# Chunked attention and a gated layer on one core: in token blocks 1 and 2, products with v and the next scores inserted as one piece

## The chip, the core and the metric

The kernel runs on one core of one Trainium2 chip. The time is that of the device, in microseconds (us); the median of three runs is given with its lowest and highest. The profile is one further execution, taken by the hardware profiler. Its span runs from the first to the last instruction that it shows. Engines are called as in the profile: PE (TensorE, matmul), PEld (its weight loads), DVE (VectorE), ACT (ScalarE), POOL (GpSimd), SP (SyncE, which issues all DMAs here).

## The reference

```python
# q, k, v: (8 batches, 8 heads, 576, 64), cut into chunks of 64 rows: plain softmax attention within each chunk
scores = scale * np.matmul(q_c, k_c.transpose(0, 1, 2, 4, 3))
scores = scores - np.max(scores, axis=-1, keepdims=True)
attn = np.exp(scores)
attn = attn / (np.sum(attn, axis=-1, keepdims=True) + 1e-09)
out = np.matmul(attn, v_c)
# x: all heads side by side, 4608 tokens x 512
gate = 1.0 / (1.0 + np.exp(-(x @ w_gate)))      # w_gate, w_val: 512 x 1536
val = x @ w_val
return (gate * val @ w_out).astype(np.float32)  # w_out: 1536 x 512
```

## The kernel before

**Work.** The 4608 tokens are nine blocks m of 512. Attention is cut into 36 units j, four to a block, and two units make a pair (j, j+1). For a pair, PE makes the scores (`products`, tile `sc`, L171), DVE takes the maximum and subtracts it (L535, L536 in `flow`), ACT takes the exponential, DVE sums and divides (L557 to L562) and transposes the 32x32 squares into `pbd` with 16 instructions (L575 in `spread`), PE multiplies by v (`values`, tile `av`, L232), and ACT copies the result out of PSUM (L243; for blocks 0 to 2 ACT and DVE split it into two parts, L250 and L251).

**Layer.** Each matmul is done in three products of high and low parts. Blocks 0, 1 and 2 go singly. For each of the 12 slices f of the hidden width, `hidden` runs 12 matmuls of the gate layer into the PSUM bank `g0` and 12 of the value layer into the bank `g1` (both are tile `g`, L262). DVE multiplies out of `g1` (L273, tile `hf`), ACT casts the product to its high part (`hh`, L275), DVE makes the low part (`hl`, L277). `down` then runs 12 matmuls of the slice before (tile `acc`, L288: four token tiles t, three matmuls each). After the last slice of a block, each token tile is copied out (`ob` or `obs`; even t on DVE, L308, odd t on ACT, L306) and stored (L309). In block 1 all four copies go through `ob`, which has two buffers: tile t=2 needs the buffer that t=0 is stored from.

Blocks 3 to 8 go in three stages n of two blocks, with seven products in place of eight for the up layers. `operands` makes the seven operands B11, B21, T1, B22, T3, T2, T4 of a stage: four differences (L401, on DVE), seven casts to the high part (L403, ACT) and seven low parts (L412, DVE; 128x1024). `first`, `middle` and `last` run the products in the PSUM tiles `cx`, `cy`, `cz` (L422); `cx` and `cy` use the banks of `acc`. A stage ends with `outward` (L503).

**Order.** On PE and DVE the code order is the order of the instructions (`manual_schedule`). ACT's and SP's is made by the framework's scheduler. The attention of pair j from 8 on is a generator, `flow`, which stops at items: a number is DVE work of that size, "S", "A" and "AS" are insertions on PE, "wait" lets at least some ticks pass. After each layer step, `rest` calls `tick` (which hands `flow` a share of DVE time, `SHARES`, and runs its DVE work up to it) and `insert` (which runs a due insertion). `step(m, f)` issues the up layers of slice f, `finish()` the down matmuls of the slice before. `due(n, k)` forces `flow` on until k operands exist.

**Insertions.** With `joined` false, the scores of pair j ("S") and the products with v of pair j-2 ("A") are two insertions at different places, all through the two PSUM banks `psa`. With `joined` true they are one ("AS"): the two `av` first, then `sc` of j into the bank `g1` (`apart`), then `sc` of j+1 into `psa`. Before the change `joined` becomes true at stage 0, which is after block 2.

Of the kernel before, what the change touches and what calls it, by code (L numbers as in the profile page):

```python
# [41 lines left out]
FIRST_PAIR = 3  # L42


SHARES = {1: 2.5, 2: 2.8, "up": 1.15, "down": 1.3}


@with_exitstack
def chunk_attn_moe(ctx: ExitStack, tc: tile.TileContext, q, k, v, w, out):
# [460 lines left out]
    def flow():  # L510


        kept = None
        for j in range(8, 4 * NB + 2, 2):
            more = j < 4 * NB
            joined = now["joined"]
            if more and joined:
                yield from spread(*kept, range(12, 16))
                yield "AS"
                values(j - 2), values(j - 1)  # L520
                scv = [products(j, True), products(j + 1)]
                load_values(j), load_values(j + 1)
            elif more:
                yield "S"
                scv = [products(j), products(j + 1)]
            if more:
                if j + 2 < 4 * NB:
                    load(j + 2), load(j + 3)
                if kept and not joined:
                    yield from spread(*kept, range(12, 16))  # L530
                pr = ap2.tile([P, 2, 8, D], F32, name="pr", bufs=1)
                for i in range(2):
                    yield 1.4
                    mx = sm.tile([P, 8], F32, name="mx")
                    nc.vector.reduce_max(out=mx, in_=scv[i], axis=AX.X)  # L535
                    nc.vector.tensor_tensor(  # L536
                        out=pr[:, i], in0=scv[i], in1=mx.unsqueeze(2).broadcast_to([P, 8, D]), op=ALU.subtract)
                pr = pr.rearrange("p u g k -> p (u g) k")
                nc.scalar.activation(pr, pr, AF.Exp, scale=0.125)
            elif kept:  # L540
                yield from spread(*kept, range(12, 16))
            if kept and not (more and joined):
                yield "A"
                values(j - 2), values(j - 1)
                if more:
                    load_values(j), load_values(j + 1)
            else:
                yield "wait"
            n, rest = divmod(j - 4 * FIRST_PAIR, 8)
            if n > 0 and rest == 0:  # L550
                yield ("open", n - 1)
                yield from operands(n - 1)
            if not more:
                return
            yield 1.5
            sums = sm.tile([P, 16], F32, name="sums2", bufs=1)
            nc.vector.reduce_sum(out=sums, in_=pr, axis=AX.X)  # L557
            nc.vector.tensor_scalar_add(out=sums, in0=sums, scalar1=1e-9)
            inv = sm.tile([P, 16], F32, name="inv2", bufs=1)
            nc.vector.reciprocal(out=inv, in_=sums)  # L560
            yield 1.2
            nc.vector.tensor_tensor(out=pr, in0=pr, in1=inv.unsqueeze(2).broadcast_to([P, 16, D]), op=ALU.mult)  # L562
            kept = pr, pbd2
            yield from spread(*kept, range(12))

    def spread(pr, pb, which):

        ps = pr.rearrange("p g (k j) -> p g k j", j=32)
        pb = pb.rearrange("p u (x c) h (i q) -> p (u x) c h i q", c=2, q=32)
        for n in which:  # L570
            c, i, h, k = n >> 3, n >> 2 & 1, n >> 1 & 1, n & 1
            src = slice((2 * c + i) * 32, (2 * c + i + 1) * 32)
            dst = slice((2 * h + k) * 32, (2 * h + k + 1) * 32)
            yield 0.44
            nc.vector.transpose(out=pb[dst, :, c, h, i, :], in_=ps[src, h::2, k, :])  # L575

    ahead = flow()
    now = dict(credit=0.0, ticks=0, since=0, unit=8, open=-1, joined=False)
    now["item"] = next(ahead)

    def advance():
        now["unit"] += 2 * (now["item"] in ("A", "AS"))
        now["item"] = next(ahead, None)
        now["since"] = now["ticks"]

    def tick(share):
        now["ticks"] += 1
        now["credit"] += share
        while now["item"] is not None:
            if isinstance(now["item"], float):  # L590
                if now["credit"] < now["item"] / 2:
                    return
                now["credit"] -= now["item"]
            elif not (now["item"] == "wait" and now["ticks"] > now["since"] + 1
                      or now["item"][0] == "open" and now["item"][1] <= now["open"]):
                break
            advance()
        now["credit"] = min(now["credit"], share)

    def insert(upto=4 * NB, pieces=0):  # L600


        if now["item"] == "S" or (
                now["item"] in ("A", "AS") and now["unit"] < upto and now["ticks"] >= now["since"] + pieces):
            advance()
# [42 lines left out]
    kept = [(p, which, c) for p in range(6) for which in range(2) for c in range(2)]  # L648
# [7 lines left out]
                keep_sums(p, which, c)  # L656

    def rest():
        for m in range(1, FIRST_PAIR):
            upto = 4 * (m + 2) if m == 1 else 4 * (m + 3)  # L660
            for f in range(2 if m == 1 else 0, NF):
                if m == 2 and f == 7:
                    now["open"] = 0
                step(m, f, "")
                tick(SHARES[m])
                insert(upto, 2)
                finish()
                tick(SHARES[m])
                insert(upto, 2)
                if m == 1:  # L670
                    keep_outer(f)
                    if f == 11:
                        keep_outer(0), keep_outer(1)

                keep(24 - len(kept), (7 * (12 * m + f - 13)) // 5)
                if m == 2:
                    if f == 8:
                        for which in range(2):
                            load_group(0, 0, which)
        for n in range(3):  # L680
            m0 = FIRST_PAIR + 2 * n
            upto = 4 * NB
            now["joined"] = True
            order = [(p, which) for p in range(6) for which in range(2)]
            due(n, 6)
            for i, (p, which) in enumerate(order):
                if i + 1 < len(order) and i > 0:
                    load_group(n, *order[i + 1])
                if pending:
                    banks[n, "z"] = sole(n, p, which)  # L690
                    while pending:
                        finish()
                first(n, p, which)
                tick(SHARES["up"] if i > 1 else 0)
                if i:
                    due(n, 7)
                    last(n, *order[i - 1])
                    tick(SHARES["up"] if i < 11 else 0)
                    insert(upto, 1)
                middle(n, p, which)  # L700
                tick(SHARES["up"] if 0 < i < 11 else 0)
                insert(upto, 1)
            load_outer(0), load_outer(1)
            parts = split(n, 0, 0)
            last(n, *order[-1])
            now["open"] = n + 1
            for b in range(2):
                for f in range(NF):
                    if f % 2 == 0:
                        later = 6 * b + f // 2 + 2  # L710
                        if later < 12:
                            load_outer(later % 6)
                        elif n + 1 < 3:
                            load_group(n + 1, 0, later - 12)
                    hh, hl = parts if f == 0 else split(n, f, b)
                    if (b, f) != (0, 0):
                        tick(SHARES["down"])
                    if (b, f) == (0, NF - 1):
                        parts = split(n, 0, 1)
                    if (n, b) == (2, 1) and f >= NF - 2:  # L720
                        pending.append((f, hh, hl))
                        continue
                    for t in range(4):
                        outward(m0 + b, f, t, hh, hl)
                    if (b, f) not in ((0, NF - 2), (0, NF - 1)):
                        insert(upto, 1)

        for i, tiles in ((0, (0, 1, 2)), (1, (0,)), (0, (3,)), (1, (1, 2, 3))):
            f, hh, hl = pending[i]
            for t in tiles:  # L730
                outward(NB - 1, f, t, hh, hl)
# [34 lines left out]
```

## Time and profile before

| | |
|---|---|
| median of 3 runs | 940.39 us (940.23 to 942.07) |
| profiled execution | 941.31 us, its span 939.5 us |
| PE busy | 924.0 us, 98% of the span, granted clock 0.993 on average |
| DVE, ACT, POOL busy | 64%, 36%, 14% |
| mean DMA traffic | 202 GB/s |

A busy PE is the sum of intervals in which a matmul is under way. They overlap, so what one more matmul costs is read from the distance of starts, not from its duration. The profile's times count from the start of the span.

### The profile page before, as it was taken

What the parts mean: (1) busy time and instruction counts of PE and PEld (TensorE: products, weight loads), DVE (VectorE), ACT (ScalarE), POOL (GpSimd) and SP (SyncE); (2) the same over time, 40 slices, a digit from 0 to 9 for tenths busy, and PEclk for the clock granted to TensorE, in tenths of its full rate; (3) what the DMA queues carried; (4) which work ended last, traced back from release to release, by engine and by line L of the source; (5) the groups of instructions that cost most, each with busy time, mean ns of one, the idle gap of its engine ahead of it and who ended that gap; (6) DMA issues with size and microseconds to landing.
All of it is one profiled execution on the core that took longest, in us unless ns stands there. A gap on an engine that the chain in (4) does not pass through costs nothing.

```text
span 939.5 us, 13059 instructions
## 1 busy us (share of the span) xinstructions
PE 924.0 (98%) x4960; PEld 762.5 (81%) x4960; DVE 602.0 (64%) x999; ACT 339.8 (36%) x554; POOL 135.1 (14%) x204
## 2 busy tenths in 40 slices
PE   6999999999999999999999999999999999999998
PEld 4788888888888888888888888888888888888886
DVE  6999973666576656866867556786866735455332
ACT  6899753233233342231323431233232421121222
POOL 1000006997069700000000000000000000000000
PEclk7999999999999999999999999999999999999999
DMA  8699885444343464576775756666656465556561
GB/s 275 219 308 293 314 297 198 135 135 129 101 153 125 139 197 157 171 227 209 232 246 201 272 201 200 199 218 223 214 202 236 165 215 185 207 176 217 211 225 45
DMA packets 81279, 189.61 MB, mean 202 GB/s; under 512 B 7488, under 2 KB 38208, under 8 KB 76608
## 3 DMA queue, kind: packets, MB, share of 16 engines
q1 hardware_dynamic: 81216, 188.77, 60.0%
q8 instruction: 39, 0.64, 0.3%
q14 instruction: 24, 0.20, 0.1%
HBM read 150.99 MB, written 37.75 MB: 201 GB/s over the span
## 4 chain that ended last, share of the span: by engine, by line
PE 87%; DVE 4%; DMA 4%; ACT 3%; issue 1%; SPq 1%; ACTq 0%; DVEq 0%
PE acc L503 21%; PE cy L422 16%; PE g L262 15%; PE cz L422 10%; PE cx L422 10%; PE acc L288 8%; PE sc L171 3%; PE av L232 3%; DMA w_raw<-w_in 3%; DMA kbd<-k_in 1%; DVE w L137 1%; DVE w_raw L132 1%; ACT w_raw L129 1%; DVE w_raw L134 1%; ACT w_raw L130 1%
## 5 line engine op out<-in xcount | busy, mean ns | idle before, releaser
L262 PE MATMUL g<-xt,w 128*128 128x512 f32 (+1 forms) x960 | 207.6, 371 | 2.3 <-ACT w L136 0.9
L262 PEld LDWEIGHTS g<-xt,w 128*128 128x128 f32 x960 | 168.5, 189 | 35.7 <-issue 1.7
L503 PE MATMUL acc<-wr,hh 128*128 128x512 f32 x576 | 178.0, 390 | 0.0
L422 PE MATMUL cy<-xc,wr 128*128 128x512 f32 x648 | 160.2, 390 | 0.0
L422 PEld LDWEIGHTS cy<-xc,wr 128*128 128x128 f32 x648 | 121.3, 188 | 25.7 <-issue 0.7
L503 PEld LDWEIGHTS acc<-wr,hh 128*128 128x128 f32 x576 | 107.7, 188 | 23.4 <-ACT hh L493 1.0
L503 PE MATMUL acc<-wr,hl 128*128 128x512 f32 x288 | 112.4, 390 | 0.0
L422 PE MATMUL cz<-xc,wr 128*128 128x512 f32 x432 | 109.7, 389 | 0.0
L422 PE MATMUL cx<-xc,wr 128*128 128x512 f32 x432 | 105.0, 389 | 0.0
L575 DVE STREAM_TRANSPOSE pbd<-pr 32x256 f32<-32x256 f32 x224 | 97.7, 436 | 4.5 <-DVE pr L562 0.5
L495 DVE TENSOR_TENSOR hl<-hid,hh 128x512 fp32r<-128x512 f32 x72 | 49.6, 690 | 72.5 <-ACT hh L493 67.5
L422 PEld LDWEIGHTS cz<-xc,wr 128*128 128x128 f32 x432 | 81.0, 188 | 17.2 <-DVE u L479 0.4
L422 PEld LDWEIGHTS cx<-xc,wr 128*128 128x128 f32 x432 | 81.0, 188 | 16.9 <-issue 0.2
L288 PE MATMUL acc<-w,hh 128*128 128x512 f32 x288 | 90.4, 395 | 0.0
L493 ACT CAST hh<-hid 128x512 fp32r<-128x512 f32 x72 | 44.6, 620 | 115.1 <-PE acc L503 84.6
L273 DVE TENSOR_TENSOR hf<-g,hf 128x512 f32<-128x512 f32 (+1 forms) x40 | 25.4, 635 | 62.8 <-PE g L262 62.7
L503 PEld LDWEIGHTS acc<-wr,hl 128*128 128x128 f32 x288 | 54.1, 188 | 12.5 <-DVE hl L495 1.3
L339 POOL TENSOR_TENSOR a_val<-w 128x256 f32<-128x256 f32 x48 | 38.4, 820 | 178.6 <-ACT hh L275 143.0
L440 DVE TENSOR_TENSOR u<-cy,s 128x512 f32<-128x512 f32 x36 | 24.9, 691 | 61.1 <-PE cy L422 61.1
L288 PEld LDWEIGHTS acc<-w,hh 128*128 128x128 f32 x288 | 52.7, 188 | 12.1 <-issue 1.7
L288 PE MATMUL acc<-w,hl 128*128 128x512 f32 x144 | 56.1, 389 | 0.0
L271 ACT ACTIVATE hf<-g 128x512 f32<-128x512 f32 (+1 forms) x40 | 22.1, 554 | 76.6 <-PE g L262 75.3
(103 smaller groups left out, 1003.5 us busy)
## 6 DMA issues: line engine op xcount, KB each, us to landing
wr<-sums SPq DMA_DIRECT2D x72, 512.0 KB, 4.5
wr<-outer SPq DMA_DIRECT2D x36, 1024.0 KB, 4.9
w_raw<-w_in SPq DMA_DIRECT2D x36, 512.0 KB, 5.8
wr<-given SPq DMA_DIRECT2D x36, 512.0 KB, 3.7
sums<-a_both SPq DMA_DIRECT2D x24, 512.0 KB, 3.5
qt<-q_in SPq DMA_DIRECT2D x36, 256.0 KB, 4.5
kbd<-k_in SPq DMA_DIRECT2D x72, 128.0 KB, 4.4
vt<-v_in SPq DMA_DIRECT2D x36, 256.0 KB, 4.3
```

The costliest lines, as they stand in the source:

```text
L171: nc.tensor.matmul(sc[c * D:(c + 1) * D, (2 * a + t) * P:(2 * a + t + 1) * P], lhsT=s["qt"][:, a, n0:n0 + D], rhs=s["kb"][:, a, :, n0:n0 + D],
L232: nc.tensor.matmul(av[a * D:(a + 1) * D, c * P:(c + 1) * P], lhsT=s["vt"][:, a, c, :], rhs=pb[:, 4 * a + c, :, :], start=True, stop=True,)
L262: nc.tensor.matmul(ps[:, tok], lhsT=wt[f, which][:, wpart, c:c + P], rhs=x[:, part, i, tok], start=n == 0, stop=n == 11)
L273: nc.vector.tensor_tensor(out=hf, in0=pv, in1=hf, op=ALU.mult)
L288: nc.tensor.matmul(acc[m, t], lhsT=hx[:, ts], rhs=wt[f, 2][:, wpart], start=f == 0 and i == 0, stop=f == NF - 1 and i == 2,)
L339: nc.gpsimd.tensor_tensor(out=val[:, 2 * n:2 * n + 2], in0=parts[:, 0], in1=parts[:, 1], op=ALU.add)
L422: nc.tensor.matmul(bank, lhsT=lhs(wpart, c), rhs=x[:, part, c], start=start and k == 0, stop=stop and k == 5, skip_group_check=True)
L440: nc.vector.tensor_tensor(out=u2, in0=y, in1=s1, op=ALU.add)
L493: nc.scalar.copy(hh, h)
L495: nc.vector.tensor_tensor(out=hl, in0=h, in1=hh.bitcast(F32), op=ALU.subtract)
L503: nc.tensor.matmul(acc[m, t], lhsT=hx[:, ts], rhs=wo[f][:, wpart], start=f == 0 and i == 0, stop=f == NF - 1 and i == 2)
L575: nc.vector.transpose(out=pb[dst, :, c, h, i, :], in_=ps[src, h::2, k, :])
```

## The change

In blocks 1 and 2, too, `flow` joins the insertions from the second pair on (the first, j = 8, has no pair ahead of it and stays an "S"). `insert` is called once per slice, between `step` and `finish`, and an insertion may follow the one before after one tick in place of two. In these blocks a "wait" is passed one tick sooner (`lag`). The share of block 1 goes from 2.5 to 2.8.

```diff
-SHARES = {1: 2.5, 2: 2.8, "up": 1.15, "down": 1.3}
+SHARES = {1: 2.8, 2: 2.8, "up": 1.15, "down": 1.3}
...
-            joined = now["joined"]
+            joined = now["joined"] and kept
...
-            elif not (now["item"] == "wait" and now["ticks"] > now["since"] + 1
+            elif not (now["item"] == "wait" and now["ticks"] > now["since"] + now["lag"]
...
     def rest():
+        now["joined"] = True
         for m in range(1, FIRST_PAIR):
...
                 step(m, f, "")
                 tick(SHARES[m])
-                insert(upto, 2)
+                insert(upto, 1)
                 finish()
                 tick(SHARES[m])
-                insert(upto, 2)
...
-            now["joined"] = True
+            now["lag"] = 1
```

On PE the six pairs j = 10 to 20 change: twelve insertions become six. The three places below are those where other engines' rows matter; numbers behind a tile's name tell instances apart.

**First place: the end of block 1.** DVE in the kernel before, from the first slice of block 2 (`g_2579`) to the second (`g_2692`); the two L308 copy out block 1's token tiles 0 and 2:

```order
L273 TENSOR_TENSOR hf<-g_2579,hf 128x512
L277 TENSOR_TENSOR hl<-hf,hh 128x512
L308 COPY ob<-acc 128x512 x2
L557 TENSOR_REDUCE sums_2647<-pr 128x16
L558 TENSOR_SCALAR sums_2647<-sums_2647 128x16
L560 RECIPROCAL inv_2650<-sums_2647 128x16
L562 TENSOR_TENSOR pr<-pr,inv_2650 128x1024
L575 STREAM_TRANSPOSE pbd<-pr 32x8x32 x7
L273 TENSOR_TENSOR hf<-g_2692,hf 128x512
```

and in the changed kernel (the same slices are `g_2545` and `g_2679`):

```order
L273 TENSOR_TENSOR hf<-g_2545,hf 128x512
L277 TENSOR_TENSOR hl<-hf,hh 128x512
L308 COPY ob<-acc 128x512 x2
L535 TENSOR_REDUCE mx<-sc 128x8
L536 TENSOR_TENSOR pr<-sc,mx 128x512
L535 TENSOR_REDUCE mx<-sc 128x8
L536 TENSOR_TENSOR pr<-sc,mx 128x512
L273 TENSOR_TENSOR hf<-g_2679,hf 128x512
```

What followed the two copies was work on `pr`; now it is the reading of the scores, the first pair of which lies in the bank `g1` that `g_2679` is to be written to. SP at this place in the changed kernel (in the kernel before, the two `vt` loads stand directly ahead of the four stores):

```order
L158 DMA vt<-v_in 128x512 x2
L149 DMA qt<-q_in 128x512
L152 DMA kbd_87<-k_in 64x2x256 x2
L149 DMA qt<-q_in 128x512
L152 DMA kbd_88<-k_in 64x2x256 x2
L309 DMA out<-ob 128x512 x4
```

Six loads of q and k for the next pair now stand ahead of the stores of block 1, too.

**Second place: the end of block 2.** DVE in the kernel before, from the low part of slice 10 to that of slice 11 and on; L412 and L401 make the operands of stage 0:

```order
L277 TENSOR_TENSOR hl<-hf,hh 128x512
L412 TENSOR_TENSOR xc<-raw,xc 128x1024
L401 TENSOR_TENSOR raw<-raw 128x2x512
L412 TENSOR_TENSOR xc<-raw,xc 128x1024
L401 TENSOR_TENSOR raw<-raw 128x2x512
L273 TENSOR_TENSOR hf<-g_3536,hf 128x512
L277 TENSOR_TENSOR hl<-hf,hh 128x512
L412 TENSOR_TENSOR xc<-raw,xc 128x1024
L308 COPY ob<-acc 128x512
L308 COPY obs<-acc 128x512
```

and in the changed kernel, from the operands behind slice 10's low part on:

```order
L412 TENSOR_TENSOR xc<-raw,xc 128x1024
L401 TENSOR_TENSOR raw<-raw 128x2x512
L412 TENSOR_TENSOR xc<-raw,xc 128x1024 x2
L401 TENSOR_TENSOR raw<-raw 128x2x512
L412 TENSOR_TENSOR xc<-raw,xc 128x1024
L401 TENSOR_TENSOR raw<-raw 128x2x512
L273 TENSOR_TENSOR hf<-g_3532,hf 128x512
L277 TENSOR_TENSOR hl<-hf,hh 128x512
L412 TENSOR_TENSOR xc<-raw,xc 128x1024
L401 TENSOR_TENSOR raw<-raw 128x2x512
L412 TENSOR_TENSOR xc<-raw,xc 128x1024
L308 COPY ob<-acc 128x512
```

Seven operand instructions, where there were four, now stand ahead of slice 11's product, and three, where there was one, between its low part and the copies. ACT there in the changed kernel, from slice 11's sigmoid to the copies of token tiles 3 and 1 (before, `obs` and `ob` stood the other way round, and the last L403 ahead of L275):

```order
L271 ACTIVATE hf<-g_3517 128x512
L403 CAST xc<-raw 128x1024 x2
L275 CAST hh<-hf 128x512
L403 CAST xc<-raw 128x1024
L306 COPY obs<-acc 128x512
L306 COPY ob<-acc 128x512
```

**Third place: the first group of stage 0.** DVE in the kernel before, from the first L440 to the second; the L412 is the low part of T4:

```order
L440 TENSOR_TENSOR u_3613<-cy,s_3605 128x512
L412 TENSOR_TENSOR xc<-raw,xc 128x1024
L557 TENSOR_REDUCE sums_3616<-pr 128x16
L558 TENSOR_SCALAR sums_3616<-sums_3616 128x16
L560 RECIPROCAL inv_3619<-sums_3616 128x16
L462 TENSOR_TENSOR u_3635<-cy,s_3605 128x512
L464 TENSOR_TENSOR hid<-cz,u_3635 128x512
L440 TENSOR_TENSOR u_3661<-cy,s_3653 128x512
```

and in the changed kernel:

```order
L440 TENSOR_TENSOR u_3613<-cy,s_3605 128x512
L462 TENSOR_TENSOR u_3629<-cy,s_3605 128x512
L464 TENSOR_TENSOR hid<-cz,u_3629 128x512
L440 TENSOR_TENSOR u_3655<-cy,s_3647 128x512
L412 TENSOR_TENSOR xc<-raw,xc 128x1024
```

The low part of T4 now stands behind the second L440. It does so at the start of stage 1 as well.

## Rows read from the trace of the kernel before

**Rows 1.** The page: PE's busy time, share of the span and instructions, and the chain that ended last, by engine.

```profile
PE 924.0 (98%) x4960; PEld 762.5 (81%) x4960; DVE 602.0 (64%) x999; ACT 339.8 (36%) x554; POOL 135.1 (14%) x204
...
PE 87%; DVE 4%; DMA 4%; ACT 3%; issue 1%; SPq 1%; ACTq 0%; DVEq 0%
```

**Rows 2.** Instructions of PE in order of time, block 1: starts of up layers (24 matmuls). Between the first two stand only the 12 down matmuls; between the second and the third two slices, with an "S" in them; between the third and the last one slice and the "A" shown. Columns: start, duration, engine, line, operation.

```profile
166.00 5.60 PE L262 MATMUL g<-xt,w 128*128 128x512 f32 x24
...
174.16 5.60 PE L262 MATMUL g<-xt,w 128*128 128x512 f32 x24
...
192.60 5.60 PE L262 MATMUL g<-xt,w 128*128 128x512 f32 x24
198.13 1.97 PE L232 MATMUL av<-pbd,vt 128*64 128x128 f32 x32
...
202.88 5.60 PE L262 MATMUL g<-xt,w 128*128 128x512 f32 x24
```

**Rows 3.** The same view in stage 0, around an "AS" (the scores are left out).

```profile
437.69 1.52 PE L422 MATMUL cy<-xc,wr 128*128 128x512 f32 x6
439.14 1.97 PE L232 MATMUL av<-pbd,vt 128*64 128x128 f32 x32
...
442.79 1.65 PE L422 MATMUL cy<-xc,wr 128*128 128x512 f32 x6
444.28 1.52 PE L422 MATMUL cz<-xc,wr 128*128 128x512 f32 x6
445.64 2.88 PE L422 MATMUL cx<-xc,wr 128*128 128x512 f32 x12
```

**Rows 4.** Instructions of DVE in order of time, block 1: the low parts of an "A" (its `av` is that of rows 2).

```profile
200.29 1.28 DVE L251 TENSOR_TENSOR xt<-av,xt 128x512 fp32r<-128x512 f32 x2
```

**Rows 5.** The end of block 1 in order of time: PE's first matmuls after the "A" and the next up layers, DVE's two copies (in brackets: idle time before, and what ended it), SP's issue of the four stores, and a maximum and subtraction of scores on DVE shortly before.

```profile
255.57 1.97 PE L232 MATMUL av<-pbd,vt 128*64 128x128 f32 x32
257.47 0.73 PE L288 MATMUL acc<-w,hh 128*128 128x512 f32 x2
...
260.32 5.60 PE L262 MATMUL g<-xt,w 128*128 128x512 f32 x24
...
258.52 0.69 DVE L308 COPY ob<-acc 128x512 f32<-128x512 f32 x1 [0.71 <-PE acc L288]
261.54 0.69 DVE L308 COPY ob<-acc 128x512 f32<-128x512 f32 x1 [2.33 <-DMA out<-ob]
262.15 1.21 DVE L557 TENSOR_REDUCE sums<-pr 128x16 f32<-128x1024 f32 x1
...
259.24 3.86 SPq L309 DMA_DIRECT2D out<-ob  x4
...
251.50 0.69 DVE L535 TENSOR_REDUCE mx<-sc 128x8 f32<-128x512 f32 x1
252.22 0.69 DVE L536 TENSOR_TENSOR pr<-sc,mx 128x512 f32<-128x512 f32 x1
```

**Rows 6.** The loads behind an "AS" of stage 0: its start on PE, SP's first and last issue; and the page's medians from issue to landing.

```profile
400.97 1.97 PE L232 MATMUL av<-pbd,vt 128*64 128x128 f32 x32
...
402.11 1.21 SPq L158 DMA_DIRECT2D vt<-v_in  x2
...
406.10 1.18 SPq L152 DMA_DIRECT2D kbd<-k_in  x2
...
kbd<-k_in SPq DMA_DIRECT2D x72, 128.0 KB, 4.4
...
out<-ob SPq DMA_DIRECT2D x22, 256.0 KB, 2.2
```

**Rows 7.** The end of block 2 in order of time: DVE from slice 10's low part on, ACT's cast and copy, and PE from the last down matmuls to the first `cx`.

```profile
353.56 0.69 DVE L277 TENSOR_TENSOR hl<-hf,hh 128x512 fp32r<-128x512 f32 x1 [0.69 <-ACT hh L275]
354.17 1.22 DVE L412 TENSOR_TENSOR xc<-raw,xc 128x1024 fp32r<-128x1024 f32 x1
...
357.70 1.22 DVE L401 TENSOR_TENSOR raw<-raw 128x1024 f32<-128x1024 f32 x1
360.35 0.69 DVE L273 TENSOR_TENSOR hf<-g,hf 128x512 f32<-128x512 f32 x1 [1.43 <-PE g L262]
...
359.00 1.05 ACT L403 CAST xc<-raw 128x1024 fp32r<-128x1024 f32 x1 [0.77 <-DVE raw L401]
361.07 0.62 ACT L275 CAST hh<-hf 128x512 fp32r<-128x512 f32 x1 [1.02 <-DVE hf L273]
365.76 0.59 ACT L306 COPY ob<-acc 128x512 f32<-128x512 f32 x1 [4.07 <-PE acc L288]
...
364.16 0.61 PE L288 MATMUL acc<-w,hh 128*128 128x512 f32 x2
...
366.88 1.52 PE L422 MATMUL cx<-xc,wr 128*128 128x512 f32 x6
```

**Rows 8.** Stage 0 in order of time: the second L440 on DVE, and on PE the product of `last` with T4 (its first six matmuls).

```profile
375.31 0.69 DVE L440 TENSOR_TENSOR u<-cy,s 128x512 f32<-128x512 f32 x1 [0.72 <-PE cy L422]
...
376.40 2.88 PE L422 MATMUL cy<-xc,wr 128*128 128x512 f32 x12
```

**Rows 9.** Block 2 on DVE in order of time, with POOL at work: from a product out of `g1` to the first transposes behind it.

```profile
284.46 0.69 DVE L273 TENSOR_TENSOR hf<-g,hf 128x512 f32<-128x512 f32 x1 [4.08 <-PE g L262]
...
291.10 3.13 DVE L575 STREAM_TRANSPOSE pbd<-pr 32x256 f32<-32x256 f32 x7 [0.46 <-DVE pr L562]
```

More of the change, by code (lines that the diff above doesn't have):

```diff
@@ L577, in chunk_attn_moe @@
     ahead = flow()
-    now = dict(credit=0.0, ticks=0, since=0, unit=8, open=-1, joined=False)
+    now = dict(credit=0.0, ticks=0, since=0, unit=8, open=-1, joined=False, lag=0)
     now["item"] = next(ahead)
```

## The prediction

> **What bounds the kernel.** First the page: PE is busy for 924.0 of 939.5 us, and the chain that ended last runs on PE for 87% of its length [rows 1]. A change gains by what it takes off PE's own line of matmuls, and loses by every wait that it puts into that line. Second, PE in order of time, for what an insertion costs now. Third, DVE, ACT and SP around the ends of blocks 1 and 2, where they have least time to spare.
>
> **Terms on PE.** One slice (24 up and 12 down matmuls) takes 174.16 - 166.00 = 8.16 us [rows 2], so 12 matmuls take 2.72. Two slices and an "S" take 192.60 - 174.16 = 18.44, so the "S" costs 18.44 - 16.32 = 2.12; a slice and an "A" take 202.88 - 192.60 = 10.28, so the "A" costs 2.12 as well. An "AS" in stage 0 stands between two groups of six matmuls, each 445.64 - 444.28 = 1.36 long: 444.28 - 437.69 - 2 x 1.36 = 3.87 [rows 3]. The joined pair saves 2 x 2.12 - 3.87 = 0.37 us, being changed into and out of once in place of twice. Six pairs: -2.2 us. The rest of PE's work stays; the "AS" that follow in stage 0 shift by some groups and cost the same there.
>
> **Copies inside the joined piece.** The scores of j+1 use the `psa` bank that the first `av` leaves. For j = 10 and 12 that `av` belongs to block 2 and is read by ACT and then by DVE (L251). Before, L251 starts 200.29 - 198.13 = 2.16 us after its `av` [rows 2, 4] and takes 1.28 for two, so the first ends about 2.8 after; the second scores would start at some three quarters of 442.79 - 439.14 = 3.65 [rows 3], 2.7 after. I take 0.2 us for each of the two, between nothing and 0.3 (DVE's low part of the slice, ahead of L251, grows when POOL is busy): +0.4.
>
> **End of block 1.** Count from the start of the first `av`, now 3.65 us ahead of the down matmuls in place of 257.47 - 255.57 = 1.90 [rows 5]. These last 260.32 - 257.47 = 2.85, the gate layer 2.72 more, so PE wants `g1` at 3.65 + 2.85 + 2.72 = 9.22. DVE has to read the first scores out of it before, and does so only behind both L308. The first L308 starts 258.52 - 257.47 = 1.05 after the down matmuls, at 4.70, and its store could go 0.72 later, at 5.42. But SP now issues the loads of q and k ahead of it; in stage 0 the same loads end 406.10 + 1.18 - 400.97 = 6.31 after the `av` [rows 6]. So the store goes at 6.35. The second L308 began 261.54 - 259.24 = 2.30 after the issue of the store whose buffer it needs [rows 5]: 8.65, if the loads ahead don't slow it. A `kbd` load lands 4.4 us after its issue, a store in 2.2 [rows 6]; the last `kbd` is issued at about 5.7 and lands between 8.0 and 10.1, and the store of 256 KB behind it a little later. I take 9.2 for the second L308 (bounds 8.65 and 10.7, the latter with a load's 4.4 us for the store), as it is nearer to the store's own row. Then 0.61 to the next instruction, 1.41 for a maximum and a subtraction (252.22 + 0.69 - 251.50): `g1` is free at 11.2, and PE stands for 2.0 us, bounds 1.5 and 3.5. Now 2.33 us of waiting for the store hold up only sums that nobody wants yet [rows 5]; that cover is gone.
>
> [...]
>
> **End of block 2.** In the times of before: slice 10's low part starts at 353.56, the operands at 354.17. Their distance is (357.70 - 354.17) / 3 = 1.18 [rows 7]. Seven in place of four end at 354.17 + 7 x 1.18 = 362.5; now slice 11's product starts at 360.35 and waits for PE, so it comes 2.1 late. ACT first casts the last difference, made at 362.5, for 1.05, then casts `hh` for 0.62: 364.2. DVE's low part 364.3 to 364.95, then low part, difference: 367.3. ACT casts that (T4) for 1.05, to 368.4, and only then copies token tile 3 for 0.59, to 369.0. The first `cx` now takes that tile's bank, and DVE's copies end as late (368.5 and 0.69). So `cx` starts at about 369.1 in place of 366.88: 2.2 us. The down matmuls before it, which want `hh` at 364.16 and the low part 0.5 later, lose 0.4 of it already. Bounds: 1.6 with operands 1.13 apart, 3.0 with 1.3.
>
> **Low part of T4.** It comes behind the second L440 now: 375.31 + 0.61 + 1.22 = 377.1 [rows 7, 8]. PE wants it at the second matmul of the product, 376.40 + 0.23. That is 0.5 us, at stage 1 as well, whose start has the same distances: +1.0, bounds 0.6 and 1.3.
>
> **Sum.** -2.2 + 0.4 + 2.0 + 2.2 + 1.0 = +3.4 us. Against the profiled execution's own 941.31 that is 944.7; that one lay 0.9 above the median, and the same difference on the median gives 943.8 us, or +0.36%. The bounds of the terms give +1.5 to +5.8 if all fall to one side.
>
> **Rivals.**
> *Both ends are hidden.* Faster: the chain ends 2.2 us earlier, 938.2. For it: the twelve separate insertions of before kept PE fed through the same places. It needs `g1` free by 9.22, so the second L308 at 7.2, less than 1 us after its store is issued, and slice 11's product at its old time with three more operands ahead. Against it are the 2.30 us and the count of seven. 8 in 100.
> *One end is hidden,* by ACT or DVE order being slacker than counted, or the store going out sooner: 1 to 1.5 us over before, 941.4 to 941.9. 20 in 100.
> *The transposes come in too large a piece.* With the higher share and the shorter wait, sums, division and 13 of 16 transposes stand between two products out of `g1`. With POOL at work the first transpose began 291.10 - 284.46 = 6.64 us after the product [rows 9]; 13 at 3.13 / 7 take 5.8, so the next product ends 6.64 + 5.8 + 0.69 = 13.1 after. PE wants the bank 8.16 + 5.44 = 13.6 after the first's matmuls, that is 13.3 after the product's start. It fits by 0.2 at worst; 0.5 us more would cost PE 0.3 in each of six pairs. With it the joined piece saves nothing: 946 to 947. 12 in 100.
> [...]
> The likeliest, the sum, has 60 in 100, with 942.4 to 945.3 as its own range.
>
> **Numbers.** About 0.2%, 1.9 us, is what a measurement of this kernel can tell from no change: same is 938.5 to 942.3. Slower: the sum's and the transposes' cases, less their lower tail, 0.68. Same: 0.22. Faster: 0.10. The range takes in the case of one hidden end and most of the transposes': 941.0 to 946.5.
>
> **What would show it.** After block 1's last slice, DVE's second L308 waits over 3 us for a store and PE's value layer (L262) then waits some 2 us for DVE's L536. At the end of block 2 PE's first `cx` waits about 2 us for ACT's L306, and slice 11's L273 starts without waiting for PE. The six joined pieces cost 3.9 us each. It is wrong if the stores overtake the loads, if ACT's order is kinder, or if waits for `g1` show up in mid-block.

## The result and the profile after

| | before | changed |
|---|---|---|
| median, runs | 942.29 us (940.23 to 943.25), 6 | 948.28 us (947.07 to 951.23), 6 |
| ratio to before | | 1.0071 (95%: 1.0058 to 1.0084) |
| profiled execution, span | 941.31 us, 939.5 us | 949.40 us, 947.6 us |

The changed kernel is slower by 0.7%. A second set of six runs, beside 23 of before, gave 949.56 us and 1.0092 (1.0073 to 1.0111). Before was slower in both sets (942.29 and 941.86 us) than in the three runs that the forecast started from.

The page of the changed kernel has the two lines that answer to [rows 1]: PE's busy time, and the chain that ended last by engine.

```profile
PE 927.8 (98%) x4960; PEld 766.3 (81%) x4960; DVE 600.4 (63%) x999; ACT 339.6 (36%) x554; POOL 134.7 (14%) x204
...
PE 95%; ACT 2%; DVE 1%; DMA 1%; issue 1%; SPq 0%; ACTq 0%; DVEq 0%
```

PE is busy for 3.8 us more with the same 4960 matmuls: some of them were slower. The waits of PE, with the total, the count and the longest one in us, show three that the kernel before does not have:

```profile
PE g L262 <- DVE pr L536: 3.6, 1, 3.6
PE cx L422 <- ACT obs L306: 1.3, 1, 1.3
...
PE cy L422 <- DVE xc L412: 0.8, 2, 0.4
```

**The end of block 1**, PE in order of time (start, duration, in brackets the idle time before and what ended it; it answers to [rows 5]): the joined insertion, the gate and value layers of block 2's second slice, the down matmuls and up layers that follow, and the next insertion.

```profile
253.18 1.97 PE L232 MATMUL av<-pbd,vt 128*64 128x128 f32 x32
254.98 1.92 PE L171 MATMUL sc<-kbd,qt 128*64 128x128 f32 x32
...
259.68 2.88 PE L262 MATMUL g<-xt,w 128*128 128x512 f32 x12
266.12 5.46 PE L262 MATMUL g<-xt,w 128*128 128x512 f32 x12 [3.57 <-DVE pr L536]
271.38 1.00 PE L288 MATMUL acc<-w,hh 128*128 128x512 f32 x2
...
274.51 5.60 PE L262 MATMUL g<-xt,w 128*128 128x512 f32 x24
...
288.20 1.97 PE L232 MATMUL av<-pbd,vt 128*64 128x128 f32 x32
```

PE stands for 3.57 us, and then the value layer takes 5.26 us to the next start, where the gate layer's duration is 2.88. The busy times of the same kernel by stretches of time (bounds and length; PE, PEld, DVE, ACT, POOL; granted clock, DMA share, GB/s) show the clock: it was 1.00 from 40 up to 264 us, and 0.50 from 266 to 272 us, behind the wait. It fell while PE still stood: from 264 to 266 us no matmul ran, and the mean clock of these 2 us is 0.84.

```profile
260.00:264.00 4.00, 2.56 (x12) 1.78 (x10) 0.04 (x1) 0.60 (x1) 0.00 (x0) 1.00 0.81 264
264.00:266.00 2.00, 0.00 (x0) 0.00 (x0) 1.97 (x4) 1.45 (x2) 0.00 (x0) 0.84 0.24 89
266.00:272.00 6.00, 5.88 (x14) 4.65 (x15) 1.58 (x3) 1.48 (x2) 4.92 (x9) 0.50 0.15 58
```

From this insertion to the next one PE takes 288.20 - 253.18 = 35.02 us. Three slices and a joined piece with nothing in their way take 3 x 8.16 + 3.87 = 28.35. So this place costs 6.7 us: 3.57 of standing, and 3.1 more. Of these, 2.5 are in the value layer (5.26 in place of 2.72 us) and 0.4 in the down matmuls (274.51 - 271.38 = 3.13 in place of 2.72). The other 0.16 come from the count: the standing is counted from the end of the gate layer's 2.88 us, where twelve matmuls take 2.72 from start to start.

DVE and SP at the same place show why `g1` was late:

```profile
257.88 0.69 DVE L308 COPY ob<-acc 128x512 f32<-128x512 f32 x1 [2.45 <-PE acc L288]
263.96 0.69 DVE L308 COPY ob<-acc 128x512 f32<-128x512 f32 x1 [5.39 <-DMA out<-ob]
264.57 0.68 DVE L535 TENSOR_REDUCE mx<-sc 128x8 f32<-128x512 f32 x1
265.29 0.69 DVE L536 TENSOR_TENSOR pr<-sc,mx 128x512 f32<-128x512 f32 x1
...
256.45 2.19 SPq L152 DMA_DIRECT2D kbd<-k_in  x2
...
259.31 1.18 SPq L152 DMA_DIRECT2D kbd<-k_in  x2
260.59 4.90 SPq L309 DMA_DIRECT2D out<-ob  x4
```

The first copy is done by about 258.6; SP gets to its store at 260.59, behind the loads (the four `kbd` are shown); the second copy starts at 263.96, 3.37 us after that issue; and only then are the scores read.

**The end of block 2** (it answers to [rows 7]): slice 11's product and the low parts on DVE, ACT's last cast and two copies, and the first `cx`.

```profile
367.36 0.69 DVE L273 TENSOR_TENSOR hf<-g,hf 128x512 f32<-128x512 f32 x1
369.08 0.69 DVE L277 TENSOR_TENSOR hl<-hf,hh 128x512 fp32r<-128x512 f32 x1 [1.03 <-ACT hh L275]
...
372.12 1.04 ACT L403 CAST xc<-raw 128x1024 fp32r<-128x1024 f32 x1 [3.07 <-issue]
373.07 0.58 ACT L306 COPY obs<-acc 128x512 f32<-128x512 f32 x1
...
373.70 1.65 PE L422 MATMUL cx<-xc,wr 128*128 128x512 f32 x6 [1.34 <-ACT obs L306]
```

DVE's product stands directly behind its operands and waits for nobody; the cast ends and the copy starts at 373.07; `cx` starts behind it.

**T4's low part** in stage 0 (it answers to [rows 8]): the second L440 and the low part on DVE, and PE's product, of which one matmul runs ahead of the wait.

```profile
382.28 0.69 DVE L440 TENSOR_TENSOR u<-cy,s 128x512 f32<-128x512 f32 x1 [1.37 <-PE cy L422]
382.89 1.22 DVE L412 TENSOR_TENSOR xc<-raw,xc 128x1024 fp32r<-128x1024 f32 x1
...
383.37 0.39 PE L422 MATMUL cy<-xc,wr 128*128 128x512 f32 x1
384.15 2.79 PE L422 MATMUL cy<-xc,wr 128*128 128x512 f32 x11 [0.40 <-DVE xc L412]
386.78 1.52 PE L422 MATMUL cz<-xc,wr 128*128 128x512 f32 x6
```

From start to start the group takes 386.78 - 383.37 = 3.41 instead of 2.72 us: 0.7, and there is a wait of the same 0.40 at stage 1.

**The joined pieces.** The first (j = 10) and the fourth (j = 16):

```profile
187.70 1.97 PE L232 MATMUL av<-pbd,vt 128*64 128x128 f32 x32
189.50 2.20 PE L171 MATMUL sc<-kbd,qt 128*64 128x128 f32 x32
191.63 0.74 PE L288 MATMUL acc<-w,hh 128*128 128x512 f32 x2
...
290.00 1.92 PE L171 MATMUL sc<-kbd,qt 128*64 128x128 f32 x32
291.84 0.73 PE L288 MATMUL acc<-w,hh 128*128 128x512 f32 x2
```

The fourth takes 291.84 - 288.20 = 3.64 us; the first 3.93, with 0.28 in the scores, which wait for the copies out of their bank.

### The profile page after: what moved, and what is told of

Same layout as the page of the kernel before. It is cut to its first block, busy times and chain, and to the rows that moved or that the text cites. A ratio compares the mean times of both kernels' runs of the same rounds, so it can differ in the third digit from the quotient of the medians.

```text
span 947.6 us, 13052 instructions
## 1 busy us (share of the span) xinstructions
PE 927.8 (98%) x4960; PEld 766.3 (81%) x4960; DVE 600.4 (63%) x999; ACT 339.6 (36%) x554; POOL 134.7 (14%) x204
## 4 chain that ended last, share of the span: by engine, by line
PE 95%; ACT 2%; DVE 1%; DMA 1%; issue 1%; SPq 0%; ACTq 0%; DVEq 0%
PE acc L503 21%; PE g L262 21%; PE cy L422 16%; PE cx L422 10%; PE acc L288 10%; PE cz L422 10%; PE sc L171 3%; PE av L232 3%; ACT early L196 1%; DMA kbd<-k_in 0%; DMA out<-ob 0%; SPq L152 0%; DVE xc L412 0%; PE tp L216 0%; ACT w_raw L129 0%
## 5 line engine op out<-in xcount | busy, mean ns | idle before, releaser
L262 PE MATMUL g<-xt,w 128*128 128x512 f32 (+1 forms) x960 | 210.4, 374 | 4.7 <-DVE pr L536 3.6
L262 PEld LDWEIGHTS g<-xt,w 128*128 128x128 f32 x960 | 170.8, 191 | 38.4 <-issue 5.3
L440 DVE TENSOR_TENSOR u<-cy,s 128x512 f32<-128x512 f32 x36 | 24.9, 692 | 55.1 <-PE cy L422 55.1
L275 ACT CAST hh<-hf 128x512 fp32r<-128x512 f32 (+1 forms) x40 | 23.1, 578 | 83.5 <-DVE hf L273 83.5
```

The lines of the kernel that those rows point to most:

```text
L262: nc.tensor.matmul(ps[:, tok], lhsT=wt[f, which][:, wpart, c:c + P], rhs=x[:, part, i, tok], start=n == 0, stop=n == 11)
L440: nc.vector.tensor_tensor(out=u2, in0=y, in1=s1, op=ALU.add)
```

## The experiments

Theory: three waits that the change makes, each at a place where the order of DVE, ACT or SP was tight, cost more than the joining saves. The costliest has two parts, PE's standing and the slow clock behind it. The rivals: the clock falls for a cause of its own; the loads ahead of the stores don't matter; the joining itself saves nothing. All kernels below are edits of the changed kernel and do the whole computation. A ratio is to the kernel before, run beside it.

**The scores read before the second copy.**

```diff
-                finish()
-                tick(SHARES[m])
+                if (m, f) == (2, 0):
+                    job = pending.pop(0)
+                    down(*job, tiles=(0, 1))
+                    tick(SHARES[m])
+                    down(*job, tiles=(2, 3))
+                else:
+                    finish()
+                    tick(SHARES[m])
```

> The changed kernel, with DVE's reading of the scores (both L535 and L536) put between block 1's two L308 copies instead of behind them. PE's matmuls and SP's loads and stores keep their order there. Theory 1 (the wait for g1 comes from DVE standing at the second L308 for the store, and the slow matmuls behind it come from that wait): PE does not wait for L536, the 24 up matmuls of block 2's slice 1 take 5.44 us from start to start instead of 11.70, the 12 down behind them 2.72 instead of 3.13: 6.7 us less, 941.6 us. Theory 2 (the slow clock there has its cause outside the wait, in the transfers or the other engines): the wait of 3.57 goes, the 3.1 us of slow matmuls stay: 944.7 us. Theory 3 (the scores are late for another reason, DVE is not what holds g1): nothing changes, 948.3 us.

Measured 943.85 us, 1.0021 (1.0008 to 1.0035). DVE now reads the scores at once, and the second copy still waits for its store, where nobody wants DVE. On PE the up layers have no wait (DVE in order of time, then PE):

```profile
261.38 0.69 DVE L308 COPY ob<-acc 128x512 f32<-128x512 f32 x1 [2.45 <-PE acc L288]
...
262.70 0.69 DVE L536 TENSOR_TENSOR pr<-sc,mx 128x512 f32<-128x512 f32 x1
...
267.09 0.69 DVE L308 COPY ob<-acc 128x512 f32<-128x512 f32 x1 [2.37 <-DMA out<-ob]
...
263.18 5.60 PE L262 MATMUL g<-xt,w 128*128 128x512 f32 x24
```

The distance to the next insertion is 28.35 us, so the whole 6.7 us of the place is gone with the wait: theory 1. The gain of 0.5 to 0.7% (4.7 to 6.7 us) against the two sets of the changed kernel fits it and excludes theory 3. Theory 2, a slow stretch that stays, is excluded for this execution by the distance; the mean clocks of all executions, further down, speak against it in general. The median lies above 941.6 for two reasons. The 6.7 us are what the place cost in one execution, and others below show less. And copies came later in this execution: DVE's low part ahead of those of j = 12 took 1.40 us in place of 0.69, and the scores waited 0.8 us for DVE's L251.

**The loads for the next pair held back.**

```diff
-                    load(j + 2), load(j + 3)
+                    if j != 14:
+                        load(j + 2), load(j + 3)
...
                 finish()
+                if (m, f) == (2, 0):
+                    load(16), load(17)
```

> The changed kernel, with the loads of q and k of units 16 and 17 issued behind the down matmuls; on SP the second q and k pair then stands behind the first two stores instead of ahead of them. SP issued that pair in 1.75 us, so the first store goes out about 1.7 us sooner, and PE's wait for g1 falls from 3.57 to about 1.9 us. If the loads ahead of the stores are a part of the cause, that is the gain, 946.6 us. If besides a wait of 1.9 us does not bring the clock down (1.34 us at the end of block 2 did not), the 3.1 us of slow matmuls go too: 943.5 us. If the loads don't matter: 948.3 us.

Measured 945.84 us, 1.003 (1.0009 to 1.0051). SP's first two stores and PE's value layer:

```profile
260.32 0.85 SPq L309 DMA_DIRECT2D out<-ob  x2
...
264.10 0.69 DVE L308 COPY ob<-acc 128x512 f32<-128x512 f32 x1 [4.46 <-DMA out<-ob]
...
266.26 2.99 PE L262 MATMUL g<-xt,w 128*128 128x512 f32 x12 [2.63 <-DVE pr L537]
```

Counted from the insertion (254.25 here) the store is issued at 6.07 us and the second copy starts at 9.85. In the five profiles that have all six loads of q and k ahead of the store it is 6.80 to 7.41 and 10.12 to 10.78 (7.41 and 10.78 in the first). So the store goes out sooner, but the copy gains only 0.3 to 0.9 us: the scheduler put just the last two `kbd` behind the first two stores, and the store then took 3.78 us to come back. And there was no fall of the clock behind a wait of 2.63 us: from 260 to 272 us it was 1.00. The loads are part of the cause, by less than expected; one profile this close to the others is weak evidence, and the last kernel below, with its stores ahead of all these loads, is the stronger.

**The wait filled with matmuls.**

```diff
+    def fill(m, f, tok, b=None):
+        b = ps_a.tile([P, TB], F32, tag="psa", name="fill"); [nc.tensor.matmul(b, ...) for _ in range(13)]
...
-        pv = up(m, f, 1, tok)
+        pv = up(m, f, 1, tok) if (m, f) != (2, 1) else fill(m, f, tok) or up(m, f, 1, tok)
```

> The changed kernel, with 13 more matmuls of 128x512 into a free PSUM bank, read by nobody, between the gate and the value layer of block 2's slice 1, where PE waits for g1. At 0.227 us each they fill 2.95 of the 3.57 us; DVE's work and the transfers stay. If PE's standing idle is what brings the clock down, the value layer's matmuls behind it run at the full rate and the kernel with more work is 3.1 us faster, 945.2 us. If the clock falls for another reason, the value layer's 12 matmuls still take 5.3 us, and the time stays at 948.3 us.

Measured 946.62 us, 1.0043 (1.0025 to 1.0062): 13 matmuls more, and 0.3 to 0.5% (2.6 to 4.6 us) less than the two sets of the changed kernel; its interval just touches that of the first set.

```profile
263.61 3.11 PE L253 MATMUL fill<-xt,w 128*128 128x512 f32 x13
267.19 2.97 PE L262 MATMUL g<-xt,w 128*128 128x512 f32 x12 [0.47 <-DVE pr L536]
```

The value layer runs at the full rate: 2.97 us, at a granted clock of 1.00 from 264 to 272 us. That speaks for the idling as the cause of the fall, but one profile does not prove it, because the next kernel idled for 3.19 us without a fall.

**The tick's wait ahead of the operands taken out.**

```diff
-            else:
+            elif j != 20:
                 yield "wait"
```

> The changed kernel without the item that makes flow wait a tick ahead of stage 0's operands: two of the operand instructions on DVE move ahead of slice 10's product, into the 6.6 us in which DVE stood idle there, so that five instead of seven stand ahead of slice 11's product, and ACT's two copies change places. Theory 1 (the operands in front of the product make cx late): slice 11's product starts 2.3 us sooner, PE waits at the first cx under 0.3 instead of 1.34 us and the down matmuls lose nothing: 1.8 to 2.2 us less, 946.2 us. Theory 2 (the last difference and its cast set cx's start, wherever the product is): under 0.5 us less.

Measured 947.29 us, 1.0049 (1.0031 to 1.0066). DVE's product of slice 11 waits for PE again, and `cx` has no wait:

```profile
363.69 0.69 DVE L273 TENSOR_TENSOR hf<-g,hf 128x512 f32<-128x512 f32 x1 [0.28 <-PE g L262]
...
370.22 1.52 PE L422 MATMUL cx<-xc,wr 128*128 128x512 f32 x6
...
267.41 2.97 PE L262 MATMUL g<-xt,w 128*128 128x512 f32 x12 [3.19 <-DVE pr L536]
```

From the last insertion to `cx` it is 370.22 - 343.32 = 26.90 us, in the changed kernel 373.70 - 344.89 = 28.81: 1.9 us, theory 1. The interval overlaps that of the changed kernel's first set, so the distance is the evidence. The edit brings forward the last difference and its cast along with the product, and ACT's two copies change places; so it shows the chain of causes and no single link of it. The third row, from the untouched end of block 1, is a surprise: a wait of 3.19 us and no fall of the clock, which was 1.00 from 264 to 272 us. The place costs 286.63 - 254.84 - 28.35 = 3.4 us there, from one insertion to the next.

**The changed kernel again.** Nothing is edited.

> The changed kernel again, unaltered, beside the next two on one chip. In its first profile the value layer behind the wait for g1 ran at half the clock; in the kernel without the tick's wait, which has a wait of 3.19 us at the same place, it did not. If the fall comes with every execution, it is there again after a wait of 3.4 to 3.6 us and the median stays at 948.3 us. If it comes in some executions only, this profile may have the wait without the fall, the boundary then costs 3.8 in place of 6.7 us, and the single times spread over 944 to 950 us with the mean clock lower in the longer ones.

Measured 949.56 us, 1.0092 (1.0073 to 1.0111). PE behind the wait, and the busy times by stretches:

```profile
270.37 4.43 PE L262 MATMUL g<-xt,w 128*128 128x512 f32 x12 [2.90 <-DVE pr L536]
...
267.00:270.00 3.00, 0.47 (x3) 0.05 (x1) 1.76 (x3) 1.83 (x3) 0.00 (x0) 1.00 0.36 137
270.00:272.00 2.00, 1.63 (x4) 1.37 (x5) 1.51 (x3) 1.06 (x2) 0.90 (x2) 0.51 0.59 218
272.00:275.00 3.00, 3.00 (x11) 2.37 (x11) 0.10 (x1) 0.64 (x1) 2.78 (x6) 0.76 0.00 0
```

The fall is there again, later and shorter, after a wait of 2.90 us and not of the 3.4 to 3.6 expected; the place costs 4.6 us (291.05 - 258.09 - 28.35) in this execution. Both profiles of this kernel have the fall, and the one of the kernel without the tick's wait, with the same order at this place, has not: the wait can pass without it, and what the fall costs differs. The mean granted clocks of single executions agree. They are 0.986 to 0.994 in the twelve of this kernel, half of them at 0.989 or less, and 0.987 to 0.999 in the ten without the tick's wait, three of them at 0.989 or less. In the 49 executions of the five edits that remove, shorten or fill the wait at this place (two of them follow) none is below 0.990; in 51 of the kernel before, one is, at 0.989. So the low means go with the wait, which speaks against a cause of its own. The clock of the first 40 us differs between executions, too (in the profiles it was 0.74 from 0 to 20 us and 0.91 from 20 to 40 us before, and 1.00 in both without the tick's wait), so no single mean shows a fall.

**The insertion behind the down matmuls.**

```diff
-                insert(upto, 1)
                 finish()
+                insert(upto, 1)
                 tick(SHARES[m])
```

> The changed kernel, with the insertion put behind the down matmuls of the slice in place of ahead of them, in all of blocks 1 and 2. The first two stores of block 1 then stand ahead of the loads on SP, and g1 is wanted 2.7 us later against the first copy. By the theory of the store and the queue PE does not wait for L536 at the end of block 1, and av's copies end before the second scores want the bank, since DVE's low part of the slice is over: each joined piece costs 3.87 us. That takes 3.8 us off, 6.7 where the clock fell, and 0.6 for the two copies; the end of block 2 and T4's low part still cost 2.2 and 0.8. 943.5 us. If scores now come too close to the value layer (from the last scores to g1's next use 2.7 instead of 5.4 us), PE waits for L536 in each of six pairs and nothing is gained: 948 us.

Measured 943.0 us, 1.0015 (1.0000 to 1.0030). PE does not wait for L536 anywhere, and all six pieces take 3.64 or 3.65 us, the first two as well. The fear of the last sentence does not come true. The first `cx` still waits 1.31 us and T4's product twice 0.40, as expected.

**All three together.** The insertion behind the down matmuls, no tick's wait ahead of the operands, and

```diff
+                if i == 1:
+                    due(n, 7)
                 first(n, p, which)
```

> The kernel of the insertion behind the down matmuls, also without the tick's wait ahead of stage 0's operands, and with T4's low part forced out ahead of the second cx of a stage. All three losses that the trace of the changed kernel shows are then undone, and only the joining is left. If the six joined pieces save 0.37 us each, PE's chain is 2.2 us shorter than before's and the kernel is faster than before by 0.2%: 940.0 us against 942.2. If joining saves nothing, or the losses have causes other than those, it is at 942 us or more.

Measured 939.47 us (937.20 to 942.11), 0.9975 (0.9961 to 0.9990): faster than before, as expected for the joining alone. None of the three waits is in its list, and PE has no other in the same stretch. Its stores go out ahead of the loads (SP and DVE at the end of block 1):

```profile
254.24 1.10 SPq L309 DMA_DIRECT2D out<-ob  x2
255.97 1.21 SPq L158 DMA_DIRECT2D vt<-v_in  x2
...
256.41 0.69 DVE L308 COPY ob<-acc 128x512 f32<-128x512 f32 x1 [1.45 <-DMA out<-ob]
...
258.45 0.69 DVE L536 TENSOR_TENSOR pr<-sc,mx 128x512 f32<-128x512 f32 x1
```

The store comes back in 256.41 - 254.24 = 2.2 us, as in [rows 5] and [rows 6]; behind loads of q and k it took 3.2 to 3.8 us in the six profiles above that have them ahead of it. In the first profile of the changed kernel the last of these loads was issued at 259.9 us and landed 3.3 us later; the store, issued at 260.59, landed 3.2 us later, 0.6 us behind the load. What holds the store up no run here shows.

## Why the prediction was right and where it was wrong

The direction and all three places were right, but 948.28 us lies above the forecast range of 941.0 to 946.5. The sum of +3.4 us was too small by 5.0 in the first profile and by 3.5 in the second, and most of that (4.7 and 2.6) lies in one term, the end of block 1.

- **Joining, -2.2 us:** right. 3.64 us inside the piece, 28.35 for three slices and a piece against 28.72 before (213.03 - 184.31, two starts of up layers behind an "S").
- **Copies inside the piece, +0.4:** too small. 0.29 us each in the first profile; 0.3 and 0.9 in the second. The bound of 0.3 did not hold where DVE's low part of the slice, ahead of L251, was slowed (1.27 us in place of 0.69 in the second profile, at j = 12). In the trace of before this instruction (L277, 128x512) takes 0.64 to 0.69 us where POOL is idle, and 0.69 to 1.77 where POOL is at work.
- **End of block 1, +2.0 (1.5 to 3.5):** this is the step that failed. The mechanism was right in each link: the second L308 waits for the store, the store stands behind the loads, the scores behind the copy. Three sizes were off. The store was issued 7.41 us after the insertion's start, not 6.35, because one pair of `kbd` issues took 2.19 us instead of the 1.18 of [rows 6]. It took 3.37 us to come back, between the two rows the prediction weighed (2.3 and 4.4). So the second copy started at 10.78, by the upper bound of 10.7 and not by the 9.2 taken, and PE stood for 3.57 us (2.90 in the second profile, with the copy at 10.12). And the step ended with the wait: it had no term for what PE does afterwards. The slow matmuls and the 0.16 added 3.1 us, in the second profile some 1.7. In place of 2.0 us the place cost 6.7 and 4.6.
- **End of block 2, +2.2 (1.6 to 3.0):** 1.9 us. The order of causes was as worked out: operands, product, cast, copy, `cx`.
- **Low part of T4, +1.0:** 1.4. The idle time was 0.40 twice, as good as forecast; but from start to start the group lost 0.7 in stage 0 and 582.99 - 579.53 - 2.72 = 0.7 in stage 1, 0.3 more than the idle time each.
- **Sum.** -2.2 + 0.6 + 6.7 + 1.9 + 1.4 = +8.4 us; the spans differ by 947.6 - 939.5 = 8.1. With the copies and the end of block 1 of the second profile it is -2.2 + 1.2 + 4.6 + 1.9 + 1.4 = +6.9. That execution's span is 950.5 us, 11.0 above before, but 4.2 of these lie ahead of the first joined piece: the up layers that start at 166.00 us in [rows 2] start at 165.85 in the first profile and at 170.20 in the second. From these up layers to the end of the span it is 773.5 us before and 781.8 and 780.3 in the two profiles: +8.3 and +6.8, as added up. Counted in the same way, the insertion behind the down matmuls is at +1.0, where joining, end of block 2 and T4 add up to +1.1, and all three together at -2.4, where only the joining's -2.2 is left.
- **The bounds.** The terms' upper bounds add up to -2.2 + 0.6 + 3.5 + 3.0 + 1.3 = +6.2, not to the +5.8 of the forecast; the first profile's +8.4 lies above either.
- **The starting point.** The forecast took the 940.39 us of three runs; before was at 942.29 with three more. Of the 4.5 us between 943.8 and 948.28, 1.9 are this.
- **The rivals.** Neither end was hidden, nor one of them. The transposes did come 13 in a piece, but no product was late for PE: behind 5.82 us of them, of which the last 8 show below, the product started the moment they were done, and PE has no wait for `g1` in mid-block.

```profile
335.98 3.58 DVE L575 STREAM_TRANSPOSE pbd<-pr 32x256 f32<-32x256 f32 x8
339.59 0.69 DVE L273 TENSOR_TENSOR hf<-g,hf 128x512 f32<-128x512 f32 x1
```

What decides whether the clock falls behind such a wait stays open: it did after 3.57 and 2.90 us, and did not after 3.19 and 2.63.

## What to carry to other kernels

A wait put into the line of the engine that is always busy can cost nearly twice its length (6.7 us for 3.57 here, but 3.4 for 3.19 in the execution without the fall), because the matmuls behind it may run at half the clock (0.50 here); so price a stall of some 3 us with that in the upper bound. When work that feeds the bound engine is moved, look at what now stands ahead of it in the reader's queue and in the queue of stores: here one copy that used to wait for a store at nobody's cost became the bound. Moving the insertion behind the matmuls whose results are being copied and stored put this place back in order; the gain of the joining was left only when the other two waits were undone as well.

## What the runs showed of the hardware that was not expected

TensorE's granted clock went from 1.00 to 0.50 in mid-kernel, behind one idle stretch of 3.57 us, and stayed there until about 272 us; behind 2.90 us it was at 0.51 for a shorter time, and behind 3.19 us in another kernel it did not fall. In the two profiles of the changed kernel it fell at different moments of the same wait: some 0.8 us before the matmuls went on in the first and 0.3 us before in the second. Both are estimates, from the mean clocks of 264 to 266 us (0.84) and of 270 to 272 us (0.51), with the fall taken as one step from 1.00 to 0.50. No run here could set the moment.

A store of 256 KB came back in 2.2 to 2.3 us where no loads of q and k stood just ahead of it on its queue, and in 3.2 to 3.8 us where they did.
